# Splitting a kernel's first loads over two DMA queues: states and half of x from ScalarE, the rest from SyncE

## The chip, the cores and the metric

One core of one Trainium2 chip. The metric is device time in microseconds (us) of one execution. A run of the unchanged kernel takes 149.7 us (149.66 to 149.92 in three runs), so differences of a tenth of a us or two are noise. Engines are named as in the profile: PE is TensorE, PEld its weight loads, DVE VectorE, ACT ScalarE, POOL GpSimd, SP SyncE; "SPq" and "ACTq" are those two engines issuing a DMA.

## The reference

Two stages. The first is attention between x (8 batches, 8 heads, 512 rows, 64 wide) and 32 state rows per head, in both directions; the second is a feed-forward block over all 4352 rows.

```python
scores  = x @ state.T / sqrt(D);  a  = softmax(scores);   xread = a @ state
scores2 = state @ x.T / sqrt(D);  a2 = softmax(scores2);  sread = a2 @ x
rows    = concat([xread, sread], axis=2)            # then (B * 544, 512)
out     = maximum(rows @ w1, rows @ w2) @ w_out     # d_model 512, d_ff 1024
```

## The kernel before

All early loads go out from SyncE, in the order of their use. `x` of batch 0 comes in two halves, even heads (`g = 0`) and odd heads (`g = 1`).

```python
def load_x(b, parts=1):
    xf_t[b] = xio.tile([128, H, NC * D], F32, tag="xf", name="xf")
    for g in range(parts):
        nc.sync.dma_start(out=xf_t[b][:, g::parts, :], in_=x[b, g::parts].rearrange("h (p c) d -> p h (c d)", c=NC))

load_states(first)            # batch 0's states, 64 KB
load_x(0, 2)                  # two halves, 512 KB each
for ch in range(2):
    load_w(w2f, moe_w2, ch)   # 1 MB
    load_wo(2 * ch)           # 512 KB each
    load_wo(2 * ch + 1)
load_w(w1f, moe_w1, 0, 2)
load_w(w1f, moe_w1, 1)
load_x(1)
...
```

TensorE's program opens with filler matmuls that keep it busy until data come. Each engine runs its program in order, so these lines are also a queue:

```python
warm_up(6)
cast_states("V", first)       # DVE casts the states
states(first)                 # PE transposes them
warm_up(9)
cast_x(0, (("A", slice(0, 4, 2)), ("V", slice(4, 8, 2)), ("P", slice(1, 4, 2)), ("V", slice(5, 8, 2))))
u_xt(0, 0, "V")               # PE transposes x's even heads
warm_up(2)
u_xt(0, 1, "A")               # PE transposes x's odd heads
...                           # scores, exp, norm; the weights' part
negate_states()               # DVE: two small negations
...
w_sub(0)                      # GpSimd: w1 - w2, 4.9 us in two pieces
w_sub(1)
```

The softmax here doesn't subtract the row's maximum and nothing guards it: scores larger than these inputs give would overflow.

## Time and profile before

| | before |
|---|---|
| median time | 149.7 us |
| span of the profiled run | 147.9 us |
| PE busy | 139.4 us, 94% of the span |
| queue q1 (SyncE) / q10 (ScalarE) | 29.56 MB / 0.13 MB |
| batch 0's states: issue to landing | 2.0 us |
| batch 0's x halves: issue to landing | 4.4 us (median of two) |

PE is busy nearly all the time, but in the first 18 us some of that is filler, so a high share there does not mean that useful work is bound by PE. The lines that matter are in the prediction below. The timeline of PE (start, length, engine, line, what):

```profile
3.85 0.41 PE L155 MATMUL ps<-ident,s_bf 128*128 128x128 bf16 x2
4.06 2.14 PE L131 MATMUL ps<-warm 128*128 128x512 bf16 x9
6.13 0.64 PE L198 MATMUL ps<-ident,xp 128*64 128x128 bf16 x16
```

The states' transposes run at 3.85 us with no idle time ahead, the nine fillers then take 2.14 us, and the even heads' transposes follow at 6.13 us.

### The profile page before, as it was taken

What the parts mean: (1) busy time and instruction counts of PE and PEld (TensorE: products, weight loads), DVE (VectorE), ACT (ScalarE), POOL (GpSimd) and SP (SyncE); (2) the same over time, 40 slices, a digit from 0 to 9 for tenths busy, and PEclk for the clock granted to TensorE, in tenths of its full rate; (3) what the DMA queues carried; (4) which work ended last, traced back from release to release, by engine and by line L of the source; (5) the groups of instructions that cost most, each with busy time, mean ns of one, the idle gap of its engine ahead of it and who ended that gap; (6) DMA issues with size and microseconds to landing.
All of it is one profiled execution on the core that took longest, in us unless ns stands there. A gap on an engine that the chain in (4) does not pass through costs nothing.

```text
span 147.9 us, 3003 instructions
## 1 busy us (share of the span) xinstructions
PE 139.4 (94%) x1228; PEld 67.4 (46%) x1249; DVE 81.7 (55%) x150; ACT 75.7 (51%) x127; POOL 44.2 (30%) x48
## 2 busy tenths in 40 slices
PE   6979899999999999999999999999999999999991
PEld 2445433434454345434443454454445434764460
DVE  5448728758887187545836581668067635721130
ACT  3175538577576268446834691477167036521011
POOL 3144269551967310640072037004100500000000
PEclk9999999999999999999999999999999999999999
DMA  4999999879999939793979497760556031502423
GB/s 75 379 387 387 387 385 340 269 138 231 262 230 307 303 68 297 273 195 118 285 226 178 177 280 188 139 284 2 106 111 284 0 75 58 226 0 70 141 89 131
DMA packets 37982, 29.89 MB, mean 202 GB/s; under 512 B 24912, under 2 KB 33360, under 8 KB 37072
## 3 DMA queue, kind: packets, MB, share of 16 engines
q1 hardware_dynamic: 37824, 29.56, 69.6%
q8 instruction: 10, 0.16, 0.4%
q10 hardware_dynamic: 144, 0.13, 0.3%
q14 instruction: 4, 0.03, 0.1%
HBM read 15.20 MB, written 8.91 MB: 163 GB/s over the span
## 4 chain that ended last, share of the span: by engine, by line
PE 74%; DMA 14%; SPq 7%; ACT 2%; issue 1%
PE acc L323 34%; PE ps L308 16%; DMA xf<-in_x_dram 11%; PE acc L319 8%; SPq L97 4%; DMA xt<-xc 3%; PE ps L280 3%; PE ps L216 2%; PE ps L367 2%; PE acc L377 2%; PE ps L239 2%; SPq L100 2%; PE acc L357 1%; ACT xc L61 1%; PE acc L375 1%
## 5 line engine op out<-in xcount | busy, mean ns | idle before, releaser
L323 PE MATMUL acc<-wo,r 128*128 128x512 bf16 x238 | 58.3, 379 | 0.5
L323 PEld LDWEIGHTS <-r 128*128 128x128 bf16 x248 | 23.9, 98 | 28.3 <-issue 0.2
L298 DVE TENSOR_SCALAR r<-ps 128x512 bf16<-128x512 f32 x32 | 22.1, 692 | 13.6 <-PE ps L308 13.6
L226 POOL TENSOR_TENSOR a<-e,er 128x512 bf16<-128x512 bf16 x14 | 14.4, 1049 | 50.5 <-ACT e L219 29.6
L308 PE MATMUL ps<-aT,swt 128*128 128x512 bf16 x127 | 29.1, 379 | 0.3 <-DVE swt L63 0.2
L63 DVE COPY ob<-acc 128x512 f32<-128x512 f32 (+1 forms) x17 | 11.0, 655 | 30.2 <-PE acc L323 29.8
L61 ACT COPY ob<-acc 128x512 f32<-128x512 f32 (+1 forms) x16 | 9.2, 573 | 28.9 <-PE acc L323 13.1
L296 ACT ACTIVATE r<-ps 128x512 bf16<-128x512 f32 x32 | 19.2, 600 | 5.8 <-PE ps L308 5.2
L308 PEld LDWEIGHTS <-swt 128*128 128x128 bf16 x128 | 12.0, 98 | 15.0 <-DVE swt L63 0.8
L319 PE MATMUL acc<-swt,aT 128*128 128x512 bf16 x56 | 16.7, 380 | 0.9 <-issue 0.8
L61 ACT CAST swt<-ps 128x512 bf16<-128x512 f32 x18 | 10.0, 588 | 13.0 <-PE ps L280 13.0
L65 POOL CAST xp<-xf 128x2048 bf16<-128x2048 f32 (+1 forms) x7 | 12.2, 1745 | 11.0 <-DMA xf<-in_x_dram 11.0
L61 ACT CAST xc<-xf 128x1024 bf16<-128x1024 f32 x12 | 11.9, 1051 | 1.6 <-DMA xf<-in_x_dram 1.6
L223 DVE TENSOR_REDUCE es<-e 128x16 f32<-128x512 bf16 x16 | 10.6, 660 | 3.6 <-ACT e L219 3.6
L63 DVE CAST swt<-ps 128x512 bf16<-128x512 f32 x18 | 11.6, 678 | 1.1 <-PE ps L280 1.1
L219 ACT ACTIVATE e<-ps 128x512 bf16<-128x512 f32 x16 | 8.8, 596 | 0.8
L131 PE MATMUL ps<-warm 128*128 128x512 bf16 x24 | 7.7, 444 | 1.3 <-POOL warm L117 1.3
L412 PE MATMUL acc<-wo,w2t 128*128 128x512 bf16 x30 | 7.3, 379 | 0.8 <-POOL wo L65 0.7
L319 PEld LDWEIGHTS <-aT 128*128 128x128 bf16 x62 | 4.7, 98 | 5.9 <-issue 2.5
L280 PE MATMUL ps<-wcat,sbd 64*32 64x512 bf16 x136 | 6.2, 383 | 0.1
L216 PEld LDWEIGHTS <-xt 128*128 128x128 bf16 x128 | 4.8, 98 | 2.8 <-ACT xt L61 0.8
L216 PE MATMUL ps<-sbd,xt 128*128 128x64 bf16 x128 | 5.3, 193 | 0.7 <-ACT xt L61 0.6
(74 smaller groups left out, 118.2 us busy)
## 6 DMA issues: line engine op xcount, KB each, us to landing
xf<-in_x_dram SPq DMA_DIRECT2D x7, 1024.0 KB, 7.6
out_dram<-ob SPq DMA_DIRECT2D x7, 1024.0 KB, 5.0
w2f<-in_moe_w_dram SPq DMA_DIRECT2D x2, 1024.0 KB, 8.9
wof<-in_moe_w_out_dram SPq DMA_DIRECT2D x4, 512.0 KB, 10.8
xf<-in_x_dram SPq DMA_DIRECT2D x2, 512.0 KB, 4.4
w1f<-in_moe_w_dram SPq DMA_DIRECT2D x2, 512.0 KB, 13.5
w1f<-in_moe_w_dram SPq DMA_DIRECT2D x1, 1024.0 KB, 14.4
out_dram<-ob SPq DMA_DIRECT2D x3, 256.0 KB, 2.2
```

Of the source, the lines that this page charges most:

```text
L61: nc.scalar.copy(o, i)
L63: nc.vector.tensor_copy(o, i)
L65: nc.gpsimd.tensor_copy(o, i)
L216: nc.tensor.matmul(p[:, k * 64:k * 64 + 64], d["xt"][:, 4 * i + 2 * g + cp, :], sbd[:, b, 2 * i + g].rearrange("p u n -> p (u n)"), start= ...
L223: nc.vector.tensor_reduce(d["es"][:, g], d["e"][:, g].rearrange("p i c n -> p (i c) n"), axis=mybir.AxisListType.X, op=ALU.add)
L226: mul.tensor_mul(d["a"][:, g].rearrange("p c i n -> p i c n"), d["e"][:, g], d["er"][:, g].rearrange("p (i c) -> p i c", i=4).unsqueeze(3) ...
L280: nc.tensor.matmul(pg[g][32 * i:32 * i + 32, :], sneg[gs, i, :] if k else sbd[gs, b, 2 * i + g, g, :], w[gs, i, ch * 512:(ch + 1) * 512], ...
L296: nc.scalar.activation(out=o, in_=p, func=ACTF.Relu)
L298: nc.vector.tensor_scalar(o, p, scalar1=0.0, scalar2=None, op0=ALU.max)
L308: nc.tensor.matmul(p, SW[b][:, g, f * 128:(f + 1) * 128], AT[b][:, g, :], start=(g == 0), stop=(g == 1))
L319: nc.tensor.matmul(OB[b][1 + c], AT[b][:, g, c * 128:(c + 1) * 128], SW[b][:, g, FF:WC], start=(g == 0), stop=False)
L323: nc.tensor.matmul(OB[b][1 + c], R[b][:, f, c * 128:(c + 1) * 128], wo[:, f, :], start=False, stop=(f == NF - 1))
```

## The change

Its intent: two sequencers issue at the same moment, so the first x half is issued half a us sooner and the states and the two halves come in side by side.

```diff
-    def load_x(b, parts=1):
+    def load_x(b, engs=(nc.sync,)):
         xf_t[b] = xio.tile([128, H, NC * D], F32, tag="xf", name="xf")
-        for g in range(parts):
-            nc.sync.dma_start(out=xf_t[b][:, g::parts, :], in_=...)
+        parts = len(engs)
+        for g, eng in enumerate(engs):
+            eng.dma_start(out=xf_t[b][:, g::parts, :], in_=...)
 ...
-    load_states(first)
-    load_x(0, 2)
+    load_states(first, nc.scalar)
+    load_x(0, (nc.sync, nc.scalar))
```

(`load_states` gets the same argument.) All other loads stay on SyncE in their order. No instruction of PE, DVE or POOL changes its place.

## The prediction

> **What bounds the kernel now.** I read three things in this order: the chain of work that ended last, to see which stage a faster load could shorten; the stretches of time with their DMA rate, to see how the loads run in that stage; and the timeline of the first 35 us, to see which arrival each engine waits for.
>
> The chain, in order of time, opens like this (start, length, what; "SPq" is SyncE issuing a DMA):
>
> ```profile
> 0.74 0.45 SPq L85
> 1.19 0.07 issue
> 1.25 0.45 SPq L80
> 1.70 0.05 issue
> 1.75 0.50 SPq L80
> 2.25 0.04 issue
> 2.29 0.51 SPq L97
> ...
> 11.39 16.16 DMA xf<-in_x_dram
> 27.55 0.02 issue
> 27.57 1.99 ACT xc L61 x2
> 29.57 0.03 ACT xp L61
> 29.59 4.50 DMA xt<-xc
> 34.10 0.04 issue
> 34.14 0.71 PE ps L216 x16
> ```
>
> The reader is to see that up to 34.1 us the end is set by loads: the first issues, then batch 1's x, then its cast and its transpose. From 34.14 us to the last copy at 144.76 us every piece of that chain but short "issue" gaps is TensorE work. So only the first 34 us can be shortened by loads, and what is gained there moves the whole rest forward, since TensorE simply starts the same work earlier.
>
> How the loads run there (busy time of each engine, granted clock, DMA share, GB/s):
>
> ```profile
> core 0: us, PE busy (x) PEld busy (x) DVE busy (x) ACT busy (x) POOL busy (x), PEclk, DMA share, GB/s
> 1.00:1.80 0.80, 0.49 (x2) 0.21 (x3) 0.57 (x1) 0.80 (x1) 0.72 (x4) 1.00 0.00 0
> 1.80:2.40 0.60, 0.60 (x3) 0.22 (x2) 0.60 (x1) 0.21 (x1) 0.15 (x1) 1.00 0.48 110
> 2.40:3.20 0.80, 0.80 (x3) 0.30 (x2) 0.74 (x2) 0.00 (x0) 0.00 (x0) 1.00 0.94 60
> 3.20:22.00 18.80, 16.75 (x174) 8.97 (x174) 9.88 (x20) 8.69 (x12) 7.09 (x8) 1.00 1.06 384
> ```
>
> Nothing moves before 1.8 us. From 1.8 to 2.4 us the 64 KB of states come, from 2.4 to 3.2 us the first x packets crawl at 60 GB/s, and from 3.2 us the 16 engines are full at 384 GB/s with no pause. The queue up to batch 1's x is 64 + 1024 (x of batch 0) + 3 x 2048 (the three weights) + 1024 (x of batch 1) = 8256 KB, or 8.45 MB; at 384 GB/s that is 22.0 us (my estimate from these rows), so it is bytes that fill this stage, and the only slack in it is the start, before 3.2 us.
>
> Which work waits for an arrival (start, length, engine, line, what; in brackets the idle time before it and who ended it):
>
> ```profile
> 5.13 0.62 ACT L61 CAST xp<-xf 128x512 bf16<-128x512 f32 x1 [3.12 <-DMA xf<-in_x_dram]
> 6.70 0.86 POOL L65 CAST xp<-xf 128x512 bf16<-128x512 f32 x1 [4.75 <-DMA xf<-in_x_dram]
> 7.62 0.64 PE L198 MATMUL ps<-ident,xp 128*64 128x128 bf16 x16 [0.31 <-POOL xp L65]
> 17.61 1.04 POOL L65 CAST wo<-wof 128x1024 bf16<-128x1024 f32 x1 [4.41 <-DMA wof<-in_moe_w_out_dram]
> 18.71 3.61 PE L412 MATMUL acc<-wo,w2t 128*128 128x512 bf16 x15 [0.72 <-POOL wo L65]
> 21.64 0.43 DVE L63 CAST w1b<-w1f 128x512 bf16<-128x512 f32 x1 [2.74 <-DMA w1f<-in_moe_w_dram]
> ```
>
> The 18.71 row is the decisive one. TensorE stood 0.72 us for the third quarter of w_out, whose cast on GpSimd waited 4.41 us for its load. Before it TensorE is ahead of the data (24 of its matmuls there are warm-up filler); after it, the w1 casts at 21.64 us, the second states' cast at 28.16 us and the transpose that lands at 34.10 us each again wait for a load, and each is tight to TensorE by 0.1 us or so.
>
> **What the Trainium skill says.** "DMA: Bandwidth & Descriptors", section "Issuing engines are not separate DMA queues": DMAs from any engine end on the same 16 DMA engines, and a second issuer only saves the sequencer's issue time. The trace agrees as far as it can: one issue lasts 0.45 to 0.56 us, and 384 GB/s is the rate already with one queue. The same page, "Queues, rings and completion order": each DMA engine takes turns, packet by packet, between the queues that have work. No run so far has two loading queues, so that is untested. "Perfetto Trace Analysis", section "DMA Instruction — HWDGE (DVE, Sync)": the descriptor generator is one block which an issuing sequencer locks for its own use. If so, an issue from ScalarE and one from SyncE at the same moment go one after the other; the trace of before cannot show it. "ScalarE: Activation LUTs", section "What ACT_TABLE_LOAD costs", has 1283 ns for the table load; this trace has 1.28 us.
>
> **The change part by part.**
>
> Removed from SyncE: the states' issue (0.45 us) and one half of batch 0's x (0.50 us). Its remaining x half can issue at 0.74 instead of 1.25 us, 0.51 us sooner, and w2's first half at about 1.25 instead of 2.29 us, 1.04 us sooner.
>
> Added to ScalarE: two issues of some 0.45 us ahead of its table load. ScalarE is free from 0.73 us; the table load of 1.28 us then runs from about 1.75 to 3.05 us. Its first real work is the cast at 5.13 us, so 2 us are left: no cost on the path.
>
> Moved on the wire: the bytes are the same. The 1.04 us on w2 are worth nothing, because by the time it could start (3.2 us) the engines are full anyway and it sits in a backlog. What counts is when x starts: in the kernel before, states first, then x, with data 1.1 us after the issue (0.74 to 1.83 for the states). With x issued at 0.74, x packets start near 1.85, beside the states; the slow first 0.8 us of x then lies from about 1.9 to 2.7, and the full rate starts near 2.7 instead of 3.2. The whole stream moves forward by up to 0.51 us.
>
> Where that goes: both x halves now share the wire, so SyncE's half (even heads) lands later than with the wire to itself, about 5.4 instead of 5.13, and the other near 5.9 instead of 6.70 (512 KB each at 384 GB/s is 1.37 us alone, 2.7 us together, from 2.7 us, plus the 0.45 us or so from last packet to start of the cast). The first costs nothing: TensorE is in nine warm-up matmuls up to 6.1 us. The second can give TensorE only the 0.31 us that it waits at 7.62. That part would be worth nothing at the end by itself, since the 0.72 us gap at 18.71 absorbs it. At 18.71 the third quarter of w_out comes 0.51 us sooner; TensorE can follow, as it is 0.31 us earlier from batch 0 and had 0.72 us to spare. The w1 casts, second states and batch 1's x shift with the stream by the same 0.51, so the path to 34.14 does too. Sum: 0 (ScalarE) + 0 (w2 earlier) - 0.51 (stream start), that is 149.7 - 0.5 = 149.2 us if the two issues really run side by side.
>
> **The rivals.**
>
> 1. One generator, ScalarE first. If issues are serialized by the lock and ScalarE's states get it first, x starts at 0.74 + 0.45 = 1.19 instead of 1.25: 0.06 us gained, 149.6 us. If SyncE gets it first, x starts at 0.74 after all and the states come 0.45 us later, landing at 0.74 + 2.0 + 0.45 = 3.2 us. That costs little: VectorE is in its memset until 2.99, its cast is 0.23 us, and TensorE is in its first six warm-up matmuls until 4.05. For the lock: the skill's page. Against: nothing in this trace.
>
> 2. The crawl at 2.4 to 3.2 us is fixed in time and not tied to the x issue. Then nothing is gained: 149.7 us. For it: the share of 0.94 at 60 GB/s says that packets wait for memory rather than for descriptors. Against: the states' packets before them did not crawl.
>
> 3. The second half of x, now on its own queue beside w2's packets, is starved and lands after 7 us. Batch 0 would slip by some tenths; but the 0.72 us gap takes up to that much, so the end stays at 149.2 to 149.7. A loss needs a slip over 0.72 us plus the stream's gain, and I see nothing of that size.
>
> 4. Batch 1's x is held by its slowest DMA engine (its 16.16 us to landing include a tail: the rate is 354 and then 326 GB/s after 22 us). If that tail depends on something other than the start, part of the 0.5 is lost at 34.14: 149.4 us.
>
> **Range and chances.** I give 0.5 us gained about 55%, next to nothing (rivals 1 and 2) about 40%, and the rest to a small loss or a larger gain: 0.55 x 0.5 + 0.4 x 0.06 = 0.3 us. Predicted 149.4 us. The range of 148.9 to 149.8 us takes in both main cases and the run-to-run spread of 0.26 us. 2% is 3 us, as much as all the time before the stream is full; gaining it is out of reach and losing it would need the gap at 18.71 to grow fivefold: 1% each, 98% within.
>
> **What would show it.** Right: SyncE's first issue at 0.74 is x; the 384 GB/s stretch starts near 2.7; odd heads' casts start near 5.9; GpSimd's cast of the third quarter at 17.1; TensorE's L216 of batch 1 at 33.6. The lock: ScalarE's or SyncE's first issue lasts about 0.9 us instead of 0.45. Wrong: the full rate still starts at 3.2; or it starts sooner and batch 1's transposed x still lands at 34.1; or the odd heads come after 7 us and the gap at 18.71 is gone.

## The result, and the profile after

The changed kernel takes 151.9 us (151.83 to 152.0, four runs), against 149.76 for the kernel before in the same rounds: 1.4% slower, ratio 1.0142 with a 95% interval of 1.0124 to 1.016. That is inside 2%, but 2.1 us above the range's top of 149.8 us. Ratios here and below are the mean time of one kernel's fast runs over that of the other's in the same rounds, so not quite the ratio of the medians quoted.

The stream did start sooner. In the changed kernel the stretch from 2.4 to 3.2 us, which the prediction shows at 60 GB/s, reads:

```profile
2.40:3.20 0.80, 0.80 (x3) 0.30 (x2) 0.59 (x1) 0.71 (x1) 0.00 (x0) 1.00 0.84 214
```

That is 214 instead of 60 GB/s. But the chain of work that ended last now begins with the half that ScalarE issued (start, length, what):

```profile
1.24 8.82 DMA xf<-in_x_dram
10.06 0.05 issue
10.12 0.87 POOL xp L65
```

That half, issued at 1.24 us, took 8.82 us to land. In the kernel before a half took 4.4 us. Chosen lines of the timeline of the changed kernel, to be read against those of before:

```profile
0.73 0.48 ACTq L86 DMA_DIRECT2D s_f<-in_state_dram  x1
0.74 0.45 SPq L81 DMA_DIRECT2D xf<-in_x_dram  x1
1.24 0.55 ACTq L81 DMA_DIRECT2D xf<-in_x_dram  x1
1.25 0.49 SPq L98 DMA_DIRECT2D w2f<-in_moe_w_dram  x1
...
4.70 0.29 DVE L63 CAST s_bf<-s_f 128x256 bf16<-128x256 f32 x1 [1.70 <-DMA s_f<-in_state_dram]
4.96 0.62 ACT L61 CAST xp<-xf 128x512 bf16<-128x512 f32 x1 [1.85 <-DMA xf<-in_x_dram]
5.05 0.40 PE L156 MATMUL ps<-ident,s_bf 128*128 128x128 bf16 x2 [0.99 <-DVE s_bf L63]
5.23 4.05 PE L132 MATMUL ps<-warm 128*128 128x512 bf16 x9
9.21 1.06 PE L199 MATMUL ps<-ident,xp 128*64 128x128 bf16 x16
10.12 0.86 POOL L65 CAST xp<-xf 128x512 bf16<-128x512 f32 x1 [8.17 <-DMA xf<-in_x_dram]
11.03 0.64 PE L199 MATMUL ps<-ident,xp 128*64 128x128 bf16 x16
...
21.33 2.98 PE L413 MATMUL acc<-wo,w2t 128*128 128x512 bf16 x13
```

Two things went wrong, and either alone would delay the odd heads' transposes to about 11 us:

- The states land late. DVE's cast starts at 4.70 us, after a wait of 1.70 us for them. PE stands still for 0.99 us, and then the same nine fillers take 4.05 us instead of 2.14, that is 427 ns from one to the next instead of some 215: half speed. The even heads' casts are done at 6.53 us (the last one is DVE's, from 6.10 us for 0.43); their transposes wait for the fillers until 9.21.
- The odd half lands late, at 10.06 us.

Why the fillers stayed slow can be read from the clock records, the stretches of PE's granted clock that the packed traces keep. Every stretch recorded there, but the last, which the end of the run cuts off, lasts a multiple of 3.413 us (before: 143.36; changed: 139.946), and the first one at full clock begins at 4.11 us before and at 10.54 us in the changed kernel. Count back from there in steps of 3.413 us. The step that ends at 4.11 us holds 0.62 us of idle PE. In the changed kernel the steps that end at 3.72 and 7.13 us hold 1.01 and 0.99 us, and the one that ends at 10.54 none. In all fourteen traces, up to the first full clock, a step with at most 0.67 us of idle PE is followed by full clock, and one with 0.94 us or more is not. So a gap counts by the step that it falls into, and where the steps lie differs from run to run.

How far does it carry? Odd heads' transposes: 7.62 to 11.03 us, 3.41 later. The group that waits for the third quarter of w_out: 18.71 to 21.33 us, 2.62 later, since the 0.72 us that PE had stood idle there is used up (3.41 - 0.72 = 2.69). Batch 1's scores: 34.14 to 36.11, 1.97 later. The span: 147.9 to 150.1, 2.2 us longer.

Queue by queue, the view of the changed kernel's DMA from 5 to 9 us shows how the half is served (packets, MB, time that the packets took as a share of 16 engines):

```profile
q1 hardware_dynamic: 506, 1.00, 69.0%
q10 hardware_dynamic: 482, 0.49, 36.8%
```

The two queues get nearly the same number of packets, but q1's are w2's 2 KB and q10's are x's 1 KB. So the half that is needed now gets a third of the bytes, and w2, which is not needed yet, gets two thirds.

From the packet records of the traces, first and last packet of each transfer (us). "Alone on ACT" and so on are the experiments below.

```
kernel                      SP: x               ACT: states         SP: w2 from   ACT: odd half
changed                     1.84 to 4.44        2.87 to 4.17        4.08          5.01 to 9.40
states alone on ACT         1.88 to 6.25 (both) 2.97 to 4.54        5.50          -
half alone on ACT           4.02 to 6.31        (SP) 1.82 to 3.53   5.39          2.05 to 4.87
w2 held back                1.86 to 4.61        2.84 to 4.34        5.53          4.17 to 6.01
half first, then states     1.87 to 4.95        5.67 to 7.61        5.13          2.64 to 5.50
```

The states' first packet came 1.0 us after x's, though both were issued within 10 ns of each other and each issue lasted under 0.5 us.

### The profile page after: what moved, and what is told of

It reads as the page before. It is cut to its first block, busy times and chain, and to the rows that moved or that the text cites. A ratio compares the mean times of both kernels' runs of the same rounds, so it can differ in the third digit from the quotient of the medians.

```text
span 150.1 us, 3024 instructions
## 1 busy us (share of the span) xinstructions
PE 143.3 (95%) x1249; PEld 67.9 (45%) x1249; DVE 80.7 (54%) x150; ACT 75.7 (50%) x127; POOL 44.0 (29%) x48
## 4 chain that ended last, share of the span: by engine, by line
PE 87%; DMA 6%; ACT 2%; DVE 1%; POOL 1%; ACTq 0%; issue 0%
PE acc L324 36%; PE ps L309 19%; PE acc L320 10%; DMA xf<-in_x_dram 6%; PE acc L413 5%; PE ps L281 3%; PE ps L368 2%; PE acc L378 2%; PE ps L217 2%; PE ps L240 2%; PE acc L358 1%; PE acc L376 1%; PE ps L402 1%; PE acc L281 1%; ACT e L220 1%; ACT xt L61 1%
## 5 line engine op out<-in xcount | busy, mean ns | idle before, releaser
L324 PE MATMUL acc<-wo,r 128*128 128x512 bf16 x248 | 59.0, 379 | 0.0
L320 PE MATMUL acc<-swt,aT 128*128 128x512 bf16 x62 | 18.1, 382 | 0.0
L132 PE MATMUL ps<-warm 128*128 128x512 bf16 x25 | 9.9, 538 | 1.3 <-POOL warm L118 1.3
```

The costliest lines, as they stand in the source:

```text
L320: nc.tensor.matmul(OB[b][1 + c], AT[b][:, g, c * 128:(c + 1) * 128], SW[b][:, g, FF:WC], start=(g == 0), stop=False)
L324: nc.tensor.matmul(OB[b][1 + c], R[b][:, f, c * 128:(c + 1) * 128], wo[:, f, :], start=False, stop=(f == NF - 1))
```

## The experiments

Two theories from the trace. Theory S: the late states cost, through PE's gap and the slow fillers. Theory B: the late half costs by itself. A rival to both is that something common to the second queue (the stream, or ScalarE's later table load) costs. Twelve experiments ran, with ten kernels (two ran a second time); all gave the right result.

### States alone on the second queue

```diff
-    load_x(0, (nc.sync, nc.scalar))
+    load_x(0, (nc.sync, nc.sync))
```

> Only the states move to the ACT queue, both x halves stay on SP. Theory S (the states land at 4.7 us on the second queue instead of about 2.7, TensorE stands still for 1 us at 4.05 and its nine warm-up matmuls then take 4.05 us instead of 2.14): the states are late here as well, so the odd heads' transposes start near 10.9 us and the time stays near 151.8 us. Theory B (only the starved x half costs): x is not split, so 149.3 to 149.7 us and the odd heads' transposes at 7.3 to 7.7 us.

151.01 us (150.12 to 151.71, four runs); ratio 1.0076, interval 1.0027 to 1.0125. Theory S holds: x is not split and it is slower all the same. PE's timeline:

```profile
5.43 0.40 PE L156 MATMUL ps<-ident,s_bf 128*128 128x128 bf16 x2 [1.37 <-DVE s_bf L63]
5.62 4.05 PE L132 MATMUL ps<-warm 128*128 128x512 bf16 x9
```

A gap of 1.37 us, then again 4.05 us for nine fillers, and the odd heads' transposes at 10.96 us although their half had long landed (its cast started at 6.89). The time was less than the 151.8 expected, and the four runs fell into two groups, 150.1 and 150.5 against 151.5 and 151.7.

### The odd half alone on the second queue

```diff
-    load_states(first, nc.scalar)
+    load_states(first)
```

> Only the odd x half moves to the ACT queue, the states stay first on SP. Theory B: the half is starved by w2's 2 KB packets as in the changed kernel, its cast starts at 9 to 10 us although the states land before 3 us and the warm-up runs without a gap; 151 to 151.8 us. Theory S: states on time, no gap, so 149.3 to 149.7 us. If the half's first packet comes about 2.1 us after its issue (as the states' did on that queue) rather than 3.8 us, it shares with the even half, lands near 7 us, and the time is 149.7.

150.4 us is the median of all four: three runs of 149.87 to 150.57 and one of 152.25, which counts as slow. Ratio of the fast ones 1.0027, interval 0.999 to 1.0063. The half was not starved: alone on its queue it went out first, its first packet came at 2.05 us and its cast started at 5.44. Now SyncE's even half was the late one, behind the states that shared the wire (cast at 6.89 us instead of 5.13). So being on the second queue is not by itself what starves a transfer. Whether standing second on it does, or w2's being under way by then, this run does not tell.

### The fillers split so that PE has no gap

```diff
-    warm_up(6)
+    warm_up(11)
     cast_states("V", first)
     states(first)
-    warm_up(9)
+    warm_up(4)
```

> The changed kernel with its 15 warm-up matmuls split 11 and 4 around the states' transposes instead of 6 and 9, so TensorE has no gap while the states are late. Theory S alone: even heads' transposes near 6.2 us instead of 9.2, 149.5 us. If the late half (theory B) is enough by itself: even heads earlier, but the odd heads' transposes still at 11.0 us (its cast at 10.1), time 151.6 to 151.9.

154.47 us (153.84 to 155.06), ratio 1.031. A miss: I expected at most 151.9. The even heads' transposes did come at 6.88 us, so the split cures theory S's delay. But the odd half landed at 10.77, and PE, with its fillers spent, stood 3.56 us until 11.74, where its 16 transposes took 1.06 us instead of 0.64. And a new cost appeared on DVE:

```profile
22.55 4.69 DVE L68 TENSOR_SCALAR sneg<-sbd 64x128 bf16<-64x128 bf16 x2
```

The two small negations took 0.38 us in the changed kernel. Here they fell beside GpSimd's subtraction, which ran from 22.35 to 27.01 us, and ended at 27.24, just after it. The clock dropped too: the clock records have half clock from 11.43 to 14.85 us.

### States on the second queue, fillers split

```diff
-    load_x(0, (nc.sync, nc.scalar))
+    load_x(0, (nc.sync, nc.sync))
...  warm_up(11) / warm_up(4) as above
```

> States on the ACT queue, both x halves on SP, warm-up split 11 and 4: both suspected causes gone, x still issued at 0.74 us. Both theories: the loss is gone; 149.3 us if the stream's start of some 0.3 us earlier is worth anything, 149.7 if not. If it stays near 151.8 both theories fall.

149.37 us (149.2 to 150.16), ratio 0.998, interval 0.995 to 1.0011. PE's timeline:

```profile
5.43 0.28 PE L156 MATMUL ps<-ident,s_bf 128*128 128x128 bf16 x2
5.55 1.03 PE L132 MATMUL ps<-warm 128*128 128x512 bf16 x4
6.51 0.76 PE L199 MATMUL ps<-ident,xp 128*64 128x128 bf16 x16
```

The states come as late as in the first experiment, 5.08 us for their cast in both, but PE is busy until then. Only the order of the fillers differs between the two, and it is worth 1.6 us on the same chip. So it is PE's gap that makes late states dear, not their lateness. The rival "something common to the second queue" falls for the states' issue; ScalarE's table load, which comes at 1.25 us here instead of 1.82, is not tested by it.

### w2 in 1 KB packets

```diff
-        load_w(w2f, moe_w2, ch)
+        # ch 0: two transfers of 256 columns each, ch 1 as before
```

> The changed kernel with w2's first 1 MB in two transfers of 256 columns, so its packets are 1 KB like x's instead of 2 KB. If the engines take turns packet by packet between the two queues, the odd half gets half the bytes rather than a third: from its first packet near 5.0 us its 32 packets per engine take 32 x (46 + 46 ns) = 2.9 us instead of 32 x (46 + 88 ns) = 4.3 us, so its cast starts near 8.6 us instead of 10.1. If its rate is limited by its own queue, the cast stays at 10.1. Time not the point: TensorE is in cold warm-ups until 9.2 anyway, 151.2 to 151.9.

The odd half's cast started at 8.73 us against an expected 8.6, and 10.12 in the changed kernel. Per queue, from 5 to 7.5 us:

```profile
q10 hardware_dynamic: 435, 0.45, 55.3%
q1 hardware_dynamic: 439, 0.43, 54.4%
```

Equal packets, and now equal bytes. So the half's rate is set by the turn-taking between queues and the size of the other queue's packets. The one run took 151.36 us (a single run, its state unknown). In it PE had a gap of 0.90 us up to 4.95, and yet its nine fillers took 2.11 us: its clock records have full clock from 4.59 us, and only 0.54 us of that gap fell into the step that ended there. They also have half clock from 11.42 to 14.83 us, so the run's time says little.

### w2 held back until 3 us

```diff
+    sbd = ...; nc.vector.memset(sbd, 0.0)        # moved up
+    nc.vector.memset(w2f[:, 0, 0:1], 0.0)        # w2's load must wait for this
     load_states(first, nc.scalar)
     load_x(0, (nc.sync, nc.scalar))
...  warm_up(11) / warm_up(4) as above
```

> The changed kernel, warm-up split 11 and 4, and a one-column memset of w2's tile on VectorE ahead of w2's load, so SyncE can issue w2 only near 3.1 us instead of 1.25. If w2 issued ahead holds the odd half back (its descriptors or its packets), the half starts right after the states, near 4.3 us or sooner, shares with x's even half only, its cast starts before 7 us: 149.3 to 150.0 us. If the half is late because it is second on the ACT queue whatever SyncE does, its first packet is still near 5.0 and its cast at 9 to 10: 151.5 or more.

149.92 us (149.29 to 150.42), ratio 1.0023, interval 0.9983 to 1.0062: as fast as before, within what can be told. The odd half's first packet came at 4.17 instead of 5.01 us, and its cast started at 6.64. From 4.5 to 5.5 us the wire was its own:

```profile
q10 hardware_dynamic: 367, 0.38, 105.5%
q1 hardware_dynamic: 13, 0.01, 2.6%
```

So two things of w2 delay the half: its packets, and about 0.8 us of the half's start, since w2 was issued ahead. Standing second on ScalarE's queue does not starve the half when w2 is held back. Both of ScalarE's issues and its late table load (1.82 us) are as in the changed kernel and nothing is lost, so the common rival falls here altogether.

### The late half with PE kept busy

```diff
...  warm_up(11) / warm_up(4) as above
     u_xt(0, 0, "V")
-    warm_up(2)
+    warm_up(18)
     u_xt(0, 1, "A")
```

> The changed kernel with warm-up split 11 and 4 and 16 more warm-up matmuls (3.5 us) between the even and the odd heads' transposes: TensorE has no gap and no cold stretch, only the late half is left. Theory B (the late half costs by itself): odd heads' transposes at 10.9 to 11.7 us, 151.2 to 152. If the half's lateness alone were harmless: 149.5. The 154.5 us of the run with the split alone I take for a second clock drop (3.6 us gap at 8.2) plus VectorE's two small negations, 2.1 and 2.5 us beside GpSimd's subtraction instead of 0.4; if those come back here, it goes over 152.

154.94 us (154.04 to 155.8), ratio 1.035. The odd heads' transposes came at 11.49 us, as expected of the late half. Beyond 152 us two things cost. One is DVE again. The kernel's DVE, then its POOL, around 21.6 us:

```profile
21.57 2.46 DVE L68 TENSOR_SCALAR sneg<-sbd 64x128 bf16<-64x128 bf16 x2
24.07 2.68 DVE L63 CAST w1b<-w1f 128x512 bf16<-128x512 f32 x1
```

```profile
21.63 4.66 POOL L387 TENSOR_TENSOR wcat<-w1f,w2f 128x1024 bf16<-128x1024 f32 x2 [0.75 <-DMA w1f<-in_moe_w_dram]
```

GpSimd's two subtractions and DVE's operations take turns as wholes. In the changed kernel the negations ran at 21.19 and the cast of w1 at 21.60 for 0.43 us, each just ahead of the subtraction at 21.62: it escaped by 0.02 us.

The other is the clock. PE waited 1.13 us for the late cast, and the clock records have half clock from 28.92 to 32.33 us. Two of the four runs, 155.74 and 155.8 us, show such a drop in their granted clock (0.989); the other two, 154.04 and 154.15 us, do not.

### Half first, states second

```diff
-    load_states(first, nc.scalar)
     load_x(0, (nc.sync, nc.scalar))
+    load_states(first, nc.scalar)
...  warm_up(15) ahead of the states' transposes, none behind
```

> The changed kernel with the order on the ACT queue turned round: odd half first, states second; all 15 warm-up matmuls ahead of the states' transposes. If the odd half starved because it stood second on its queue behind the states with w2 already issued, it now starts near 2.1 us, both halves are cast from 5.4 to 6.2 us, the states come last near 6 us: 149.5 to 150.3 us. If a second queue is starved as such: half's cast after 8 us, over 151.

154.92 us (154.04 to 154.95), ratio 1.0335: a miss in time, but the half behaved as expected. It started at 2.64 us, and both halves were cast from 5.62 and 6.14 us on. Now the states were second on their queue. Their 64 KB started at 5.67 us and was not cast before 8.28. I had expected them near 6. DVE, which runs in order, held its share of x's casts behind that cast, PE lost its clock again, and a cast of w2 took 2.56 us beside the subtraction. With w2 issued ahead, the starved one is whichever stands second on ScalarE's queue.

### The same, with DVE kept out of GpSimd's way

```diff
...  warm_up(11) / warm_up(4) and warm_up(18) as above
-            negate("V", sneg[gs], ...)
+            negate("P", sneg[gs], ...)
-    for e, i in (("P", slice(0, 1)), ("A", slice(1, 2)), ("V", slice(2, 3)), ("A", slice(3, 4))):
+    for e, i in (("P", slice(0, 1)), ("A", slice(1, 2)), ("A", slice(2, 3)), ("A", slice(3, 4))):
```

> The run with 18 warm-up matmuls between even and odd heads again, but the two small negations on GpSimd and VectorE's one w1 cast on ScalarE, so that VectorE has no copy out of SBUF while GpSimd does its 4.7 us subtraction at 21.6 us. If the excess over the changed kernel in that run (154.9 against 151.9) was VectorE shut out during that subtraction (its three small operations took 2.46 and 2.68 us instead of 0.4), it goes: 151 to 152 us, and that is the price of the late half by itself. If it stays above 153.5, something else costs.

152.44 us (152.07 to 152.47), ratio 1.0171, interval 1.0153 to 1.019. The odd heads' transposes at 11.17 us, PE busy and fast throughout, DVE free of the subtraction: 2.5 us less than the run with 18 fillers (154.94). Some 1.7 us of that is the clash itself, against the two runs there at full clock (154.04 and 154.15); the rest is the clock drop that only the other two had. What is left, 2.6 us over the kernel before, is the late half by itself as far as this run isolates it, 0.4 more than the top of my estimate. Part of that may be the experiment's own cost, since GpSimd spends 1.44 us on the negations at 14.04 us.

### A second look at the states alone

No edit.

> The run with only the states on the ACT queue, unchanged, for a second look, since its four times lay at 151.7, 150.1, 150.5 and 151.5. If its two clusters are the TensorE clock after the gap: a time near 151.6 goes with nine warm-ups of about 4.05 us as in the first look, a time near 150.3 with about 2.1 us (as in the run with small packets, where a gap of 0.9 us left the clock up).

151.29 us (a single run, state unknown), with nine fillers in 4.05 us. It fits the slow group, but the fast group was not caught in a profile, so that its runs are the ones whose clock came up in time remains a guess.

### The kernel before with the fillers split

```diff
-    warm_up(6) ... warm_up(9)
+    warm_up(11) ... warm_up(4)
```

> Control: the kernel before with its warm-up split 11 and 4. Its states land before 3 us, so there is no gap to close; TensorE reaches the states' transposes later but x's even heads at 6.2 to 6.5 us. 149.6 to 149.9 us, same as before. If it gains as much as the states-on-ACT run (149.4), that gain was the split and not the earlier start of x.

149.76 us, ratio 1.0002, interval 0.9989 to 1.0016. The split alone does nothing when the states are on time.

### States on the second queue, fillers split, five rounds

No edit.

> The run with the states alone on the ACT queue and the split warm-up again, with five rounds, to settle whether it beats the kernel before: 149.3 to 149.5 us, ratio 0.997 to 0.999. Its stream is full some 0.3 us sooner; if the interval reaches over 1, the earlier start bought nothing that can be told.

149.61 us (149.45 to 149.91), ratio 0.9993, interval 0.9978 to 1.0008. It does not beat the kernel before in a way that can be told. That is a little over the 149.3 to 149.5 expected. The interval allows a gain of 0.3 us at most for the earlier start of x (0.9978), and none; no version that ran beats the kernel before in a way that can be told. In this trace full clock begins only at 6.29 us, and the run still took 149.82 us: PE was busy with fillers until then.

## Why the prediction was wrong

Taken by its own steps:

- **Bytes and the stream's start.** Right in kind, and too large. The 214 GB/s show it, so rival 2 falls, but from 1.8 to 2.4 us the rate was 56 instead of 110 GB/s: the lead at 3.2 us is 91 KB, or 0.24 us at 384 GB/s (an estimate from these stretches). Batch 1's x had its first packet at 21.76 us instead of 21.97 (packet records): 0.21 us gained of the 0.51. It was worth nothing, since ScalarE came to cast that x at 28.34 us instead of 27.57, with no wait for DMA: its own late work set the path, not the load.
- **ScalarE's two issues and its table load.** Right: 0.48 and 0.55 us, the table load at 1.82, and the first cast at 4.96 waited for data.
- **The late states: "That costs little".** This is the first step that failed, in its size. The main sum has nothing for the states, which were to come beside x; the first rival has them land at 3.2 us. The states landed near 4.7 us: their first packet came 1.0 us after x's and then took turns with x's packets. I had given that slack correctly as ending at 4.05, when the six fillers end. What I had not priced is what lies beyond: with a gap of 0.99 us in PE's first 5 us the next nine fillers cost 4.05 instead of 2.14 us. The first and fourth experiments show the effect; their difference is 1.6 us of run time.
- **"the other near 5.9".** This is the second step that failed. I let the two halves share the wire from 2.7 us and put w2 behind both. But w2 is behind only the half on its own queue. The odd half began at 5.01 us, 0.57 us after the even half's last packet, and shared with w2 by packets, 1 KB against 2 KB. It landed at 10.06.
- **Rival 3, the starved half.** The mechanism was named; its size was taken as "some tenths" and dismissed with "I see nothing of that size". The sharing could have been sized from the durations in the packet records of before: 32 packets per engine, each behind a w2 packet, at 46 + 88 ns is 4.3 us. From the start at 5.0 us, which only the run showed, that gives 9.3 us; the last packet came at 9.40. The late half by itself is 2.6 us of run time.
- **"the 0.72 us gap at 18.71 absorbs it".** It did take up its share: 3.41 became 2.62 there. It was just too small. The prediction's last sign of being wrong, odd heads after 7 us and that gap gone, is what came. That the time still fell within 2% is luck as far as the argument goes: a loss was to need this gap to grow, and it came from work ahead of it.
- **The lock on the descriptor generator.** Predicted to show as an issue of 0.9 us; it did not, all four first issues lasted 0.45 to 0.55. The packets came one transfer after the other all the same: 1.0 us later for the second queue when 512 packets of x led (0.7 to 1.1 over all runs of that kind), and 0.2 us later when 256 packets of states led. That fits one generator that works through the transfers in turn, but no run here shows the generator itself, and the second figure fits it less well.

The two costs overlap rather than add: late states alone about 1.3 us (1.8 to 2.0 in the slow group), the late half by itself 2.6 us, both together 2.1 us. Each alone brings the odd heads' transposes to about 11 us, so the second costs nothing on top of the first.

"TensorE: Matmul & The Clock Gate", section "Part 1: The HAM clock gate", states that the array starts at half clock and rises after about 3.4 us of sustained activity, judged in a free-running window, so that the moment varies from run to run. These traces agree: 427 and some 215 ns between fillers, the steps of 3.413 us above, and a gap of 0.9 us that did no harm to the fillers in one run, beside 0.99 and 1.37 us that did. "SBUF — State Buffer", section "SBUF: two separate sides", states that DVE in certain modes and GpSimd take a shared port pair as an exclusive lock for a whole instruction. That is how the 2.46, 2.68 and 4.69 us above read, and casts out of PSUM beside the subtraction in the changed kernel kept their 0.69 us.

## What to carry to other kernels

In these runs a second DMA queue was not a way past the first one's backlog: it took turns with it packet by packet, so small urgent rows lost to large patient ones, and what stood second on it, with w2 issued ahead, waited longer than it would have in line (the odd half's cast at 10.12 against 6.70 us). Before moving a load, ask what else will be on the wire when it gets there, and not only when it is issued. Where filler matmuls bridge a wait, put them ahead of the first instruction that can block, and after moving anything by a us or two, check which of DVE's copies now fall beside a long GpSimd operation.

## What the Trainium skill lacked or had wrong

- "DMA: Bandwidth & Descriptors", "Issuing engines are not separate DMA queues": a second issuer is said only to save the sequencer's issue time. Here it also changed who gets the wire: 506 packets and 1.00 MB against 482 packets and 0.49 MB, and the same 512 KB landed after 8.82 instead of 4.4 us. The page has the turn-taking by packets elsewhere, but not that bytes then follow packet size.
- Same page, no section: the first packet of a second queue came 1.0 us after the first queue's (2.87 against 1.84 us), although both were issued at 0.73 to 0.74.
- "Perfetto Trace Analysis", "DMA Instruction — HWDGE (DVE, Sync)": the wait for the generator's lock is said to lie in the profiled interval. Issues at the same moment on two engines lasted 0.45 and 0.48 us, against 0.45 us for the first issue alone in the kernel before: no such wait shows.
- "TensorE: Matmul & The Clock Gate", "HAM oscillation — how this bites in real kernels", names idle gaps over some 3.4 us as the danger, and no section says how much idle time one window may hold and still count as busy. Here 0.99 us in one step of 3.413 us kept the array slow (nine fillers took 4.05 instead of 2.14 us) while 0.67 us did not, and in the run with 1 KB packets the clock fell back to half at 11.42 us though no gap after its rise was longer than 1.36 us.
- No page says that the granted clock in the profile's views is 1.00 where the trace has no clock record: it read 1.00 in the stretches from 1 to 22 us of the changed kernel, slow fillers included, though its first record, of full clock, begins at 10.54 us.
